# Second channel weights stored block by block from ScalarE, and the gated unit's spatial products one batch ahead of its output products, all on 128 rows

## The chip, the cores and the metric

The kernel runs on one core of a Trainium2 chip. The metric is the device time of one execution in microseconds (us). A core has TensorE (PE, with PEld for its weight loads), VectorE (DVE), ScalarE (ACT), GpSimd (POOL) and SyncE (SP, whose queue here issues DMAs). PEclk is the clock granted to TensorE, as a share of its upper level of 2.4 GHz; the lower level is 1.2 GHz, 0.5 in the rows.

## The reference, cut to what matters

Causal attention over 4 batches, 12 heads, 448 positions of 64, then a token and channel mixer with residuals, then a gated unit whose spatial product runs over the positions. Biases and weights are inputs; the five large weights arrive in 64 bits.

```python
attn = softmax(mask(q @ k.T / 8)) @ v                  # (4, 12, 448, 64)
x = attn.transpose(0, 2, 1, 3).reshape(4, 448, 768)
u = x + (relu(x.T @ w_tok1) @ w_tok2).T                # token mixing, 448 -> 256 -> 448
y = u + relu(u @ w_ch1) @ w_ch2                        # channel mixing, 768 -> 1536 -> 768
h = relu(y @ w_in)                                     # 768 -> 1024
g, v = h[..., :512], h[..., 512:]
v = (v - mean(v)) / sqrt(var(v) + 1e-6)
v = einsum('ts,bsd->btd', w_spatial, v) + b_spatial[None, :, None]
return (g * v) @ w_out                                 # 512 -> 768
```

## The kernel before, in words

**Numbers in two parts.** From the channel mixer on (and from the third batch of attention on), each factor is kept as a rounded high part and a low part that holds the rest (`split`, L78: the high part mostly on ScalarE, the low part on VectorE or GpSimd), and a product is three matmuls into one PSUM bank: high by high, high by low, low by high (`mm3`, L114, whose matmuls stand at L118 to L120). A 64-bit weight block is turned to 32 bits by three VectorE steps (`narrow_steps`, L99, steps at L103, L105 and L107).

**The scheduled part, L783 to L796.** Attention (24 pairs of heads, `pair_jobs`, 6 to a batch), token mixing (8 groups, `group_jobs`), the preparation of the channel weights (`weight_jobs`), the channel mixer (`channel_jobs`, one call to a batch) and the loads of the gated unit's input weights (`win_jobs`) are written as jobs with an engine, a cost, predecessors and a rank. `emit` (L213) is a list planner: it always takes the job that can start first by its own reckoning, and of those the one of lowest rank, and writes it out; each engine then runs its jobs strictly in that order. The table `RK` (L259) holds the rank offsets by kind of job, and `lag` (L261) the time that the planner puts between a job and its successor on another engine. So a change of any cost, rank or lag can reorder every engine.

**Weight blocks.** There are 24: 12 of `w_ch1` and 12 of `w_ch2`, each 128 x 768 numbers. One is loaded, narrowed by VectorE (tile `wn`), split by GpSimd (high part at L70, low part at L76) and stored to device memory, from which `channel_jobs` loads it again (tile `wb`, L670) once for each batch. `wn` and `wb` tiles share four slots (bank `w`: G4, G5, D2, D3). A `w_ch1` block is stored by one DMA (L622). A `w_ch2` block holds 128 rows of the hidden dimension and every output column, while the product wants 768 rows and 128 columns: so it is stored by two DMAs that scatter it in pieces of 512 bytes (L626), and a `wb` block of the second product waits for all six stores of its half (`src`, L673). The order of preparation is all of `w_ch1`, then all of `w_ch2`. Loads and stores all stand in SP's queue.

**Channel mixer.** For each batch and each half of the 1536 hidden columns there are six blocks of the first product (`cps<-uhl,wb`) and six of the second (`cps<-hid,wb`), each of 18 matmuls. In the first two batches' time the attention of the other two runs between these blocks.

**Gated unit, L802 to L951.** For each batch: four tiles of gate products (`psg`), then the value products of the three 128-row chunks (`value`, L818); after every second batch also one `value` call for the 64-row chunks of two batches together. Each value is normalised into `vn`. After the last batch, `normed(b)` (L885) splits the normalised values of a batch into high and low parts, `spatial(b)` (L903) multiplies them by the spatial weights (4 tiles of 11 matmuls), adds the bias and multiplies by the gate (L912, L913) and splits the result (`ghl`), and `project(b)` (L920) makes the output products (6 tiles of 12 matmuls) and stores them. The loop at L946 takes `spatial(b)`, `normed(b + 1)`, `project(b)` in turn. In `spatial` the 64-row chunk takes two matmuls: L908 multiplies a 128-row tile that has the high part in one half of its rows and the low part in the other by the high weights, which stand twice; L909 multiplies the high half alone, 64 rows, by the low weights. This part is written in program order, and the framework's own scheduler sets the order on each engine.

Of the kernel before, what the change touches and what calls it, by code (L numbers as in the profile page):

```python
# [16 lines left out]
DM = H * D  # L17
# [5 lines left out]
FF = 512  # L23
NG = FF // 128
CHUNKS = [(0, 64), (64, 192), (192, 320), (320, 448)]
MASKED = -1.0e9
# [5 lines left out]
def mixer_kernel(ctx: ExitStack, tc: tile.TileContext, qkv, wtok, w12, winu, winv, wsp, wout, bsp, out):  # L32
# [226 lines left out]
    RK = dict(s=39.4, q=-0.8, v=-43.0, e=22.5, pn=-59.8, f=5.8, hl=-47.5, pv=-27.9, ue=48.3, ut=-36.6, x=-71.7, h=56.7, hr=26.4, u=48.9, uc=37.6, us=19.6, ld=-6.7, ch=68.9, hd=-132.8, ad=33.2, nw=38.1, nh=39.6, wi=75.5)  # L259

    def lag(a, b):  # L261
        return 0.0 if a == b else 220.0 if a == "PE" else 80.0
# [326 lines left out]
    w2d = [dram.tile([KM, 128, 2, 6, 128], F32, tag=f"w2_{i}", name=f"w2_{i}") for i in range(2)]  # L589

    def weight_jobs(prev2):

        order = list(prev2)
        for x in range(2 * NF):
            i, f = x // NF, x % NF
# [8 lines left out]
            for s in range(3):  # L604
# [7 lines left out]
                at = Job("DVE", (900, 1500, 1350)[s], step, after=[at], rank=r + RK["nw"], bank=None if first else "w")  # L612
# [26 lines left out]
    def channel_jobs(b):  # L639
# [14 lines left out]
        for half_ in range(2):  # L654
# [6 lines left out]
            for x in range(12):  # L661
# [6 lines left out]
                def load(me, one=one, f=f, d=d, cell=cell, h=half_):  # L668
                    t = slot(me.tile, [2, DM], F32R, "wb")
                    nc.sync.dma_start(t.bitcast(F32), w1d[f] if one else w2d[h][d].rearrange("p t f c -> p t (f c)"))  # L670
# [172 lines left out]

    gates = []
    DO = {}
    for b in range(B):
# [10 lines left out]
        gates.append(g)  # L857
        for c in (1, 2, 3):
# [4 lines left out]
        if b == 0:  # L863
            for i in range(2):
                t = slot(f"D{turn('dbl', 4)}", [2 * S], F32, "wspt")
                nc.sync.dma_start(t, wsp[:, 2 * S * i : 2 * S * i + 2 * S])
                for c in range(2):
                    split(wsps[0][2 * i + c], wsps[1][2 * i + c], t[:, c * S : c * S + S], lo_eng="pool")
# [5 lines left out]
        if b == 3:  # L874
            for i in range(2):
                narrow(gates[2 + i][:, 4:6, :].rearrange("p f s -> p (f s)")[:, :DM], DO[1][i])
# [3 lines left out]
    for f in range(NG):  # L880
        t = slot(w12_slot(3 * (f // 2) + 1 + f % 2), [2, DM], F32R, f"wohl{f}")
        split(t[:, 0, :], t[:, 1, :], gates[f][:, 4:6, :].rearrange("p f s -> p (f s)")[:, :DM], lo_eng="pool")
        wo.append((t[:, 0, :], t[:, 1, :]))

    def normed(b):  # L885
        ns = []
        o = slice(64 * (b % 2), 64 * (b % 2) + 64)
        lo = slice(64 - 64 * (b % 2), 128 - 64 * (b % 2))
        t = slot(w12_slot(7), [3, FF], F32R, "nsh")
        x = vns[b // 2, 0]  # L890
        split(t[o, 0, :], t[lo, 0, :], x[o])
        ns.append((t[:, 0, :], t[o, 0, :]))
        ts = [t[:, 1, :], t[:, 2, :]]
        t = slot(w12_slot(8), [3, FF], F32R, "n8")
        ts += [t[:, i, :] for i in range(3)]
        t = slot(w12_slot(10), [3, FF], F32R, "n10")
        ts.append(t[:, 0, :])
        for c in (1, 2, 3):
# [119 lines left out]
```

## Time and profile before

| what | value |
|---|---|
| median of 3 runs | 902.36 us (901.5 to 902.97) |
| the profiled execution | 903.91 us, span 902.1 us, mean granted clock 0.987 |
| TensorE busy, share of the span | 863.0 us, 96% |
| VectorE, ScalarE, GpSimd busy | 423.8 us (47%), 300.7 us (33%), 284.1 us (31%) |
| TensorE's share of the chain that ended last | 80% |
| DMA | 148.65 MB, mean 165 GB/s |

The span runs from the first to the last instruction; the execution's own time holds 1.8 us more around it. Matmuls are pipelined, so TensorE counts as busy from the start of one to its modelled end, and a short pause between two matmuls can vanish in the busy time; the step from one matmul's start to the next shows it. The program has clear stages, so the tables by stage say more than the shares of the whole.

### The profile page before, as it was taken

What the parts mean: (1) busy time and instruction counts of PE and PEld (TensorE: products, weight loads), DVE (VectorE), ACT (ScalarE), POOL (GpSimd) and SP (SyncE); (2) the same over time, 40 slices, a digit from 0 to 9 for tenths busy, and PEclk for the clock granted to TensorE, in tenths of its full rate; (3) what the DMA queues carried; (4) which work ended last, traced back from release to release, by engine and by line L of the source; (5) the groups of instructions that cost most, each with busy time, mean ns of one, the idle gap of its engine ahead of it and who ended that gap; (6) DMA issues with size and microseconds to landing.
All of it is one profiled execution on the core that took longest, in us unless ns stands there. A gap on an engine that the chain in (4) does not pass through costs nothing.

```text
span 902.1 us, 12716 instructions
## 1 busy us (share of the span) xinstructions
PE 863.0 (96%) x4768; PEld 739.5 (82%) x4768; DVE 423.8 (47%) x775; ACT 300.7 (33%) x816; POOL 284.1 (31%) x376
## 2 busy tenths in 40 slices
PE   7899999886997999999999999999999999989998
PEld 5576777775996899989889999999998888877877
DVE  3787857754455334333452352322244355364342
ACT  5766565433323323333342201110204133322111
POOL 3589776646164231323313010101003000331020
PEclk9999999997999999999999999999999999999999
DMA  4686776877577855554255367677753000001111
GB/s 146 186 278 220 235 201 226 263 229 242 172 215 253 264 179 195 200 178 171 79 197 159 132 211 248 217 255 253 250 175 111 1 1 0 1 21 41 62 62 62
DMA packets 62701, 148.65 MB, mean 165 GB/s; under 512 B 17200, under 2 KB 40368, under 8 KB 62640
## 3 DMA queue, kind: packets, MB, share of 16 engines
q1 hardware_dynamic: 62640, 147.84, 49.9%
q8 instruction: 38, 0.62, 0.3%
q14 instruction: 23, 0.19, 0.1%
HBM read 123.44 MB, written 24.38 MB: 164 GB/s over the span
## 4 chain that ended last, share of the span: by engine, by line
PE 80%; DVE 6%; DMA 6%; POOL 4%; ACT 2%; issue 1%; SPq 0%; POOLq 0%; ACTq 0%; DVEq 0%
PE cps L118 13%; PE cps L120 12%; PE cps L119 12%; PE pst L405 4%; PE sa L350 3%; DMA w<-wn 3%; PE psg L120 2%; PE psg L119 2%; PE psg L118 2%; POOL pbig L392 2%; PE pso L436 2%; PE psv L118 2%; PE psv L119 2%; PE psv L120 2%; PE pso L119 2%; PE pso L120 2%
## 5 line engine op out<-in xcount | busy, mean ns | idle before, releaser
L118 PE MATMUL cps<-uhl,wb 128*128 128x448 f32 x288 | 109.4, 380 | 6.4 <-DMA wb<-w 2.9
L118 PE MATMUL cps<-hid,wb 128*128 128x448 f32 x288 | 108.8, 378 | 4.2 <-DMA wb<-w 4.2
L120 PE MATMUL cps<-hid,wb 128*128 128x448 f32 x288 | 106.5, 370 | 0.0
L119 PE MATMUL cps<-hid,wb 128*128 128x448 f32 x288 | 106.3, 369 | 0.0
L119 PE MATMUL cps<-uhl,wb 128*128 128x448 f32 x288 | 106.1, 368 | 0.0
L120 PE MATMUL cps<-uhl,wb 128*128 128x448 f32 x288 | 106.0, 368 | 0.0
L392 POOL TENSOR_SCALAR pbig<-pbig,rcp 128x448 f32<-128x448 f32 (+1 forms) x96 | 61.5, 650 | 108.6 <-DVE rcp L383 103.1
L83 DVE SCALAR_TENSOR_TENSOR hid<-cps,hid 128x448 fp32r<-128x448 f32 x48 | 29.9, 623 | 102.9 <-ACT hid L705 102.9
L377 ACT ACTIVATE pbig<-sa,nm 128x448 f32<-128x448 f32 (+1 forms) x72 | 42.6, 596 | 93.4 <-DVE nm L370 63.3
L713 DVE TENSOR_TENSOR U<-cps,U 128x448 f32<-128x448 f32 x48 | 29.9, 623 | 85.7 <-PE cps L120 85.1
L76 POOL TENSOR_TENSOR winl<-win,winh 128x1536 fp32r<-128x1536 f32 x4 | 14.8, 3695 | 171.4 <-ACT winh L68 139.5
L705 ACT ACTIVATE hid<-cps 128x448 fp32r<-128x448 f32 x48 | 26.1, 544 | 118.5 <-PE cps L120 118.5
L370 DVE TENSOR_REDUCE nm<-sa 128x2 f32<-128x896 f32 (+1 forms) x72 | 46.6, 679 | 38.8 <-PE sa L358 37.9
L118 PEld LDWEIGHTS cps<-uhl,wb 128*128 128x128 f32 x288 | 54.8, 190 | 12.1 <-issue 3.5
L118 PEld LDWEIGHTS cps<-hid,wb 128*128 128x128 f32 x288 | 54.9, 191 | 8.8 <-DMA wb<-w 4.3
L120 PEld LDWEIGHTS cps<-hid,wb 128*128 128x128 f32 x288 | 54.8, 190 | 4.7
L119 PEld LDWEIGHTS cps<-hid,wb 128*128 128x128 f32 x288 | 54.9, 191 | 4.3
L120 PEld LDWEIGHTS cps<-uhl,wb 128*128 128x128 f32 x288 | 54.6, 190 | 4.6
L119 PEld LDWEIGHTS cps<-uhl,wb 128*128 128x128 f32 x288 | 54.8, 190 | 3.8
L405 PE MATMUL pst<-ident,pbig 128*128 128x128 f32 x288 | 49.0, 282 | 4.6 <-POOL pbig L392 4.5
L76 POOL TENSOR_TENSOR wn<-wn 128x768 fp32r<-128x768 f32 x24 | 44.0, 1832 | 1.8
L392 POOL TENSOR_SCALAR psml<-psml,rcp 64x64 f32<-64x64 f32 (+1 forms) x96 | 43.2, 460 | 0.0
(184 smaller groups left out, 1951.7 us busy)
## 6 DMA issues: line engine op xcount, KB each, us to landing
wb<-w SPq DMA_DIRECT2D x96, 768.0 KB, 4.5
dbl<-in_w SPq DMA_DIRECT2D x24, 768.0 KB, 5.9
stage<-in_qkv SPq DMA_DIRECT2D x24, 448.0 KB, 4.1
w<-wn SPq DMA_DIRECT2D x12, 768.0 KB, 5.5
w<-wn SPq DMA_DIRECT2D x24, 384.0 KB, 8.2
out_t<-out SPq DMA_DIRECT2D x24, 224.0 KB, 1.9
dbl<-in_winu SPq DMA_DIRECT2D x4, 768.0 KB, 6.1
dbl<-in_winv SPq DMA_DIRECT2D x4, 768.0 KB, 6.8
```

Source lines behind the costliest of these rows:

```text
L76: e.tensor_tensor(lo, x, hi.bitcast(F32), op=ALU.subtract)
L83: nc.vector.scalar_tensor_tensor(lo, x, 0.0, hi.bitcast(F32), op0=ALU.max, op1=ALU.subtract)
L118: nc.tensor.matmul(ps, ah, bh, start=(first and i == 0), stop=False)
L119: nc.tensor.matmul(ps, ah, bl, start=False, stop=False)
L120: nc.tensor.matmul(ps, al, bh, start=False, stop=(last and i == n - 1))
L350: nc.tensor.matmul(out, x[rows, q0:q1], y[rows, S : 2 * S][:, ks[j]], start=(t == 0), stop=False, skip_group_check=True)
L370: nc.vector.tensor_reduce(nm[:M], S_.ps[:M, :, o : o + W], axis=mybir.AxisListType.X, op=ALU.max, negate=True)
L377: nc.scalar.activation(P(n, i)[:M, j, :], S_.ps[:M, j, o : o + W], AF.Exp, bias=SM[n, i][:M, j : j + 1], scale=1.0, accum_out=sums[n % 2][ ...
L392: nc.gpsimd.tensor_scalar(x, x, rcp[n % 2][:M, 2 * ((i - 1) % 4) + j :][:, 0:1], 1.0, op0=ALU.mult, op1=ALU.mult)
L405: nc.tensor.transpose(me.ps[:, o : o + M], src(), ident[:M, :M])
L705: nc.scalar.activation(part(x, 0), first.ps, AF.Relu)
L713: nc.vector.tensor_tensor(U[b][:, d, :], first.ps, U[b][:, d, :], op=ALU.add)
```

## The change

In `weight_jobs` the input layout of `w_ch2` is rearranged on the host so that a block already is what the second product wants (768 rows by 128 columns). Each `w_ch2` block is stored by one DMA like the others and a `wb` block waits for its own store alone. The blocks are prepared in the order six of `w_ch1`, six of `w_ch2`, six, six. All stores move from SP's queue to ScalarE's. The planner gets other costs, ranks and lags.

In the gated unit the 64-row matmul of L909 becomes one of 128 rows: its weights `wz` hold the low part in the half that belongs to the batch and zeros in the other. `normed(0)` moves ahead of the last batch's values and uses other slots; the loop becomes `spatial(0)`, `spatial(1)`, `project(0)`, `spatial(2)`, `project(1)`, `spatial(3)`, `project(2)`, `project(3)`; `project` no longer starts its first two tiles together.

```diff
+NARROW = (980, 1150, 1160)
-    RK = dict(s=39.4, q=-0.8, v=-43.0, e=22.5, pn=-59.8, f=5.8, hl=-47.5, pv=-27.9, ue=48.3, ut=-36.6, x=-71.7, h=56.7, hr=26.4, u=48.9, uc=37.6, us=19.6, ld=-6.7, ch=68.9, hd=-132.8, ad=33.2, nw=38.1, nh=39.6, wi=75.5)
+    RK = dict(s=53.0, q=-0.3, v=14.0, e=26.8, pn=-68.2, f=43.8, hl=-6.2, pv=-11.9, ue=33.0, ut=-111.3, x=-99.8, h=59.1, hr=-23.0, u=59.0, uc=55.2, us=45.6, ld=-58.4, ch=71.8, hd=-31.0, ad=-6.0, nw=76.8, nh=72.7, wi=295.1)
     def lag(a, b):
-        return 0.0 if a == b else 220.0 if a == "PE" else 80.0
+        return 0.0 if a == b else 220.0 if a == "PE" else 1500.0 if a in ("SP", "Q") else 80.0
...
-            i, f = x // NF, x % NF
+            i, f = x // 6 % 2, x % 6 + 6 * (x // NF)
...
-                if i == 0:
-                    nc.sync.dma_start(w1d[f], cell["w"].bitcast(F32))
-                else:
-                    for t in range(2):
-                        dst = w2d[f // 6][:, :, t, f % 6, :].rearrange("d p c -> p d c")
-                        nc.sync.dma_start(dst, cell["w"][:, t, :].bitcast(F32).rearrange("p (d c) -> p d c", c=128))
-            job(("st", i, f), "SP", 3300, store, after=[lo], rank=r + RK["nh"]).uses(first)
+                nc.scalar.dma_start((w1d, w2d)[i][f], cell["w"].bitcast(F32))
+            at2 = Job("ACT", 80, store, after=[lo], rank=r + RK["nh"])
+            job(("st", i, f), "Q", 3000, lambda _: None, after=[at2], rank=r + RK["nh"]).uses(first)
...
-                src = [("st", 0, f)] if one else [("st", 1, 6 * half_ + y) for y in range(6)]
+                src = [("st", 0, f)] if one else [("st", 1, 6 * half_ + d)]
-                L = job(("ld", b, i), "SP", 3300, load, after=[*src, *gate], rank=r + RK["ld"], bank="w")
+                L = job(("ld", b, i), "SP", 2500, load, after=[*src, *gate], rank=r + RK["ld"], bank="w")
...
+    wz = slot("q0", [2, S], F32R, "wz")
+    nc.gpsimd.memset(wz.bitcast(F32), 0.0)
...
+        tags = (w12_slot(7), w12_slot(8), w12_slot(10)) if b % 2 else ("D2", "D3", "D0")
...
+        if b == 3:
+            for i in range(2):
+                narrow(gates[2 + i][:, 4:6, :].rearrange("p f s -> p (f s)")[:, :DM], DO[1][i])
+            ns0 = normed(0)
...
-            nc.tensor.matmul(ps, ns[0][1][:, c], wsps[1][0][o], start=False, stop=False)
+            nc.tensor.matmul(ps, ns[0][0][:, c], wz[:, b % 2, :], start=False, stop=False)
...
-    ns = normed(0)
-    for b in range(B):
-        gs = spatial(b, *ns)
-        if b + 1 < B:
-            ns = normed(b + 1)
-        project(b, gs)
+    ns1 = normed(1)
+    gs = spatial(0, ns0)
+    split_out()
+    ns0 = normed(2)
+    gs1 = spatial(1, ns1)
+    project(0, gs)
+    ns1 = normed(3)
+    gs = spatial(2, ns0)
+    project(1, gs1)
+    gs1 = spatial(3, ns1)
+    project(2, gs)
+    project(3, gs1)
...
-    w12[:, :, DM:] = c2.reshape(NF, 128, DM)
+    w12[:, :, DM:] = c2.reshape(2, 6, 128, KM, 128).transpose(0, 3, 2, 1, 4).reshape(NF, 128, DM)
```

SP's queue of the kernel before, where the first half's second product begins in the first batch (`stage` is the next pair's attention input, `dbl` a 64-bit block, `wn` a prepared block, `w2_0` the stored `w_ch2` blocks of the first half, `wb` a block loaded again):

```order
L626 DMA w2_0_130<-wn_1945 128x6x128 x2
L93 DMA dbl_2199<-in_w12 128x1536
L286 DMA stage_84<-in_qkv 64x64
L287 DMA stage_84<-in_qkv 64x64
L294 DMA stage_84<-in_qkv 128x384
L282 DMA stage_84<-in_qkv 128x896
L626 DMA w2_0_130<-wn_2044 128x6x128 x2
L670 DMA wb_2260<-w2_0_130 128x1536
L670 DMA wb_2291<-w2_0_130 128x1536
```

The same place in SP's queue of the changed kernel:

```order
L94 DMA dbl_2095<-in_w12 128x1536
L667 DMA wb_2125<-w1_5_123 128x1536
L94 DMA dbl_2146<-in_w12 128x1536
L667 DMA wb_2181<-w2_0_130 128x1536
L94 DMA dbl_2214<-in_w12 128x1536
L667 DMA wb_2246<-w2_1_131 128x1536
L287 DMA stage_84<-in_qkv 64x64
L288 DMA stage_84<-in_qkv 64x64
L295 DMA stage_84<-in_qkv 128x384
L667 DMA wb_2295<-w2_2_132 128x1536
```

Before, the first load of a second-product block stands right behind the sixth store that it needs; in the change no store stands in this queue, the loads wait for one store each, and the 64-bit blocks stand between them.

ScalarE's order in the changed kernel before the channel mixer's first product (`qk` is the split of pair 12's scores' inputs, U a copy of attention's output, `xs` and `hid` are token mixing):

```order
L622 DMA w2_5_135<-wn_1392 128x1536
L622 DMA w1_6_124<-wn_1461 128x1536
L69 CAST qk_1550<-stage_84 128x896
L464 COPY U1_81<-pso_1521 128x448
L479 CAST xs_102<-psn_1567 64x128
L480 CAST xs_102<-psn_1567 128x3x128
L519 ACTIVATE hid_104<-psh_1561 128x384
L519 ACTIVATE hid_104<-psh_1588 128x384
```

Two stores now stand ahead of pair 12's split, where ScalarE had none. 18 of the 24 stores stand ahead of the first split of the channel mixer's input in this queue. In the same way VectorE narrows 18 blocks ahead of the low parts of that input where it narrowed 16, and GpSimd prepares 13 blocks ahead of pair 12's probabilities where it prepared 15.

ScalarE's order in the gated unit before (`ghl` is the split of a gated tile, `nsh` and `n8` are the next batch's `normed`, `out` the copies of output tiles):

```order
L68 CAST ghl_7057<-gt_7054 128x448
L68 CAST ghl_7075<-gt_7072 128x448
L68 CAST nsh_7114<-vn_6548 64x512
L68 CAST nsh_7114<-vn_6442 128x512
L68 CAST ghl_7093<-gt_7090 128x448
L68 CAST n8_7117<-vn_6442 128x512 x2
L68 CAST ghl_7111<-gt_7108 128x448
L942 COPY out_7151<-pso_7125 128x448
```

The same place in the change:

```order
L69 CAST ghl_7111<-gt_7108 128x448
L69 CAST ghl_7152<-gt_7149 128x448
L69 CAST ghl_7170<-gt_7167 128x448
L69 CAST nsh_7301<-vn_6994 64x512
L69 CAST nsh_7301<-vn_6768 128x512
L69 CAST ghl_7188<-gt_7185 128x448
L69 CAST n8_7304<-vn_6768 128x512
L69 CAST n8_7304<-vn_6994 128x512
L69 CAST ghl_7206<-gt_7203 128x448
L942 COPY out_7222<-pso_7209 128x448
```

Before, the first output tile follows the splits of its own batch; in the change the splits of the next batch (`ghl_7152` to `ghl_7206`) stand between.

## Rows read from the trace of the kernel before

**Rows 1.** Busy us, instructions, granted clock and DMA by stage.

```profile
core 0: us, PE busy (x) PEld busy (x) DVE busy (x) ACT busy (x) POOL busy (x), PEclk, DMA share, GB/s
0.00:174.24 174.24, 159.99 (x1004) 116.31 (x1004) 126.60 (x202) 103.24 (x332) 121.23 (x173) 1.00 0.69 219
174.24:300.00 125.76, 109.77 (x657) 96.48 (x657) 61.57 (x100) 38.71 (x113) 58.72 (x76) 0.92 0.74 226
300.00:671.70 371.70, 371.70 (x2108) 339.01 (x2107) 132.57 (x251) 96.36 (x252) 70.10 (x106) 1.00 0.58 196
671.70:788.75 117.05, 117.05 (x542) 101.37 (x541) 54.00 (x151) 39.48 (x78) 17.33 (x11) 1.00 0.09 30
788.75:898.40 109.65, 104.52 (x465) 86.36 (x464) 48.40 (x72) 22.87 (x43) 16.70 (x11) 0.98 0.13 49
```

**Rows 2.** TensorE's waits, 174 to 301 us (us in total, times, longest).

```profile
PE cps L118 <- DMA wb<-w: 7.1, 5, 4.2
PE sa L350 <- ACT psml L377: 3.4, 1, 3.4
```

**Rows 3.** The waits of SP's queue, whole span.

```profile
SPq L670 <- DMA w<-wn: 62.2, 13, 9.0
SPq L622 <- POOL wn L76: 6.7, 3, 4.9
```

**Rows 4.** DMA issues (KB each, median us to landing).

```profile
w<-wn SPq DMA_DIRECT2D x12, 768.0 KB, 5.5
w<-wn SPq DMA_DIRECT2D x24, 384.0 KB, 8.2
```

**Rows 5.** The stretches of low clock, columns as in rows 1.

```profile
190.00:195.00 5.00, 4.20 (x14) 3.83 (x15) 2.75 (x4) 1.93 (x8) 2.62 (x5) 0.66 0.33 84
215.00:230.00 15.00, 10.45 (x48) 9.47 (x49) 2.98 (x6) 2.28 (x11) 6.83 (x11) 0.57 0.56 199
290.00:300.00 10.00, 8.90 (x48) 7.28 (x47) 2.65 (x5) 3.21 (x6) 3.88 (x6) 0.83 0.96 284
```

**Rows 6.** Timeline of TensorE, spatial products of batch 0 (start us, us, instruction [idle before]).

```profile
790.72 0.52 PE L908 MATMUL psp<-hw,nsh 128*128 128x448 f32 x1 [1.79 <-DVE nsh L76]
...
797.55 0.37 PE L908 MATMUL psp<-hw,nsh 128*128 128x448 f32 x1
797.85 0.46 PE L909 MATMUL psp<-hw,nsh 64*128 64x448 f32 x1
...
798.55 0.37 PE L119 MATMUL psp<-hw,nsh 128*128 128x448 f32 x1
```

**Rows 7.** Timeline of TensorE, end of the last output products.

```profile
890.11 0.36 PE L120 MATMUL pso<-ghl,wohl 128*128 128x448 f32 x1
...
898.03 0.37 PE L120 MATMUL pso<-ghl,wohl 128*128 128x448 f32 x1
```

**Rows 8.** TensorE's waits, 788 to 903 us.

```profile
PE pso L119 <- DVE ghl L76: 3.3, 6, 0.6
```

**Rows 9.** Groups of instructions, 788.7 to 898.4 us (count, busy us, mean ns, idle before).

```profile
L913 DVE TENSOR_TENSOR gt<-gt,gate 128x448 f32<-128x448 f32 x16 | 13.2, 827 | 0.4
L76 DVE TENSOR_TENSOR ghl<-gt,ghl 128x448 fp32r<-128x448 f32 x16 | 12.9, 807 | 7.0 <-ACT ghl L68 7.0
L912 DVE TENSOR_TENSOR gt<-psp,bias 128x448 f32<-128x448 f32 x16 | 10.0, 625 | 10.8 <-PE psp L120 10.0
```

**Rows 10.** The weight blocks' own steps (duration ns min/median/max, first and last start).

```profile
L103 DVE TENSOR_SCALAR wn<-dbl x24: 549/666/4283, 40.3 to 283.7; 128x768 uint32<-128x768 uint32 x24
L105 DVE SCALAR_TENSOR_TENSOR wn<-dbl,wn x24: 942/960/2443, 40.9 to 285.4; 128x768 uint32<-128x768 uint32 x24
L70 POOL TENSOR_SCALAR wn<-wn x24: 821/830/1528, 43.3 to 290.9; 128x768 fp32r<-128x768 f32 x24
L76 POOL TENSOR_TENSOR wn<-wn x24: 1800/1826/1993, 44.2 to 291.8; 128x768 fp32r<-128x768 f32 x24
```

**Rows 11.** The `w_ch1` stores on SP's queue (duration of an issue as in rows 10).

```profile
L622 SPq DMA_DIRECT2D w<-wn x12: 326/384/1192, 47.1 to 135.7; - x12
```

More of the change, by code (lines that the diff above doesn't have):

```diff
@@ L588, in mixer_kernel @@
     w1d = [dram.tile([128, 2, DM], F32, tag=f"w1_{f}", name=f"w1_{f}") for f in range(NF)]
-    w2d = [dram.tile([KM, 128, 2, 6, 128], F32, tag=f"w2_{i}", name=f"w2_{i}") for i in range(2)]
+    w2d = [dram.tile([128, 2, DM], F32, tag=f"w2_{i}", name=f"w2_{i}") for i in range(2 * KM)]
     def weight_jobs(prev2):
@@ L610, in step @@
                     next(cell["g"])
-                at = Job("DVE", (900, 1500, 1350)[s], step, after=[at], rank=r + RK["nw"], bank=None if first else "w")
+                at = Job("DVE", NARROW[s], step, after=[at], rank=r + RK["nw"], bank=None if first else "w")
                 if first:
@@ L842, in value, with normed @@
         vns[key] = vn
+    wz = slot("q0", [2, S], F32R, "wz")
+    nc.gpsimd.memset(wz.bitcast(F32), 0.0)
+    def normed(b):
+        o = slice(64 * (b % 2), 64 * (b % 2) + 64)
+        lo = slice(64 - 64 * (b % 2), 128 - 64 * (b % 2))
+        tags = (w12_slot(7), w12_slot(8), w12_slot(10)) if b % 2 else ("D2", "D3", "D0")
+        t = slot(tags[0], [3, FF], F32R, "nsh")
+        x = vns[b // 2, 0]
+        split(t[o, 0, :], t[lo, 0, :], x[o])
+        ns = [(t[:, 0, :],)]
+        ts = [t[:, 1, :], t[:, 2, :]]
+        t = slot(tags[1], [3, FF], F32R, "n8")
+        ts += [t[:, i, :] for i in range(3)]
+        t = slot(tags[2], [3, FF], F32R, "n10")
+        ts.append(t[:, 0, :])
+        for c in (1, 2, 3):
+            split(ts[2 * c - 2], ts[2 * c - 1], vns[b, c], lo_eng="pool")
+            ns.append((ts[2 * c - 2], ts[2 * c - 1]))
+        return ns
     gates = []
@@ L873, in mixer_kernel, with split_out, spatial @@
             DO[1] = [fetch(half(wout[:, 1, :], i)) for i in range(2)]
-        if b == 3:
-            for i in range(2):
-                narrow(gates[2 + i][:, 4:6, :].rearrange("p f s -> p (f s)")[:, :DM], DO[1][i])
     wo = []
[L880 to L898, printed above, removed]
-            split(ts[2 * c - 2], ts[2 * c - 1], vns[b, c], lo_eng="pool")
-            ns.append((ts[2 * c - 2], ts[2 * c - 1]))
-        return ns, o
-    def spatial(b, ns, o):
+    def split_out():
+        for f in range(NG):
+            t = slot(w12_slot(3 * (f // 2) + 1 + f % 2), [2, DM], F32R, f"wohl{f}")
+            split(t[:, 0, :], t[:, 1, :], gates[f][:, 4:6, :].rearrange("p f s -> p (f s)")[:, :DM], lo_eng="pool")
+            wo.append((t[:, 0, :], t[:, 1, :]))
+    def spatial(b, ns):
         gs = []
@@ L920, in project @@
     def project(b, gs):
-        def products(ps, m, fs):
+        for m in range(KM):
+            ps = bank(4 + turn("v", 4), "pso")[:, :S]
             c = slice(128 * m, 128 * m + 128)
-            mm3(ps, [(wo[f][0][:, c], wo[f][1][:, c], *gs[f]) for f in fs], first=fs[0] == 0, last=fs[-1] == NG - 1)
-        pss = [bank(4 + turn("v", 4), "pso")[:, :S] for _ in range(2)]
-        for fs in (range(NG - 1), range(NG - 1, NG)):
-            for m in range(2):
-                products(pss[m], m, fs)
-        for m in range(KM):
-            if m < 2:
-                ps = pss[m]
-            else:
-                ps = bank(4 + turn("v", 4), "pso")[:, :S]
-                products(ps, m, range(NG))
+            mm3(ps, [(wo[f][0][:, c], wo[f][1][:, c], *gs[f]) for f in range(NG)])
             if m % 3 == 0:
```

11 lines of the change are left out of this document (9 added, 2 removed).

## The prediction

> **What bounds the kernel now.** I read the table by stage first [rows 1]. The bounds are where TensorE changes its work: at 174.24 us the first channel product starts, at 671.70 the first gate product, at 788.75 the last value product is over. From 300 to 788.75 us TensorE is busy without a gap at the full clock, and 489 of the 902 us can only change with the number of products, which the change leaves as it is there. The reader is to see that the time to be had lies in three other stretches. In 174.24 to 300 TensorE stands for 125.8 - 109.8 = 16.0 us, and its clock is 0.92. In 788.75 to 898.4 it stands for 5.1 us at 0.98. In 0 to 174.24 it stands for 14.2 us, while VectorE is busy 127, GpSimd 121 and ScalarE 103 of 174 us: there no engine is full, and attention's chain through all four sets the pace.
>
> Then I read who is waited for. In the second stretch it is mainly reloaded weights, and attention's single score bank: scores waited 3.4 us for ScalarE to read the scores ahead of them [rows 2]. SP's queue stood 62.2 us in 13 places at a reload until a store had landed [rows 3]. Six `w_ch2` blocks went out in 12 scattered half stores of 8.2 us each, where a whole `w_ch1` block takes 5.5 [rows 4].
>
> **The gated unit's end, term by term.** A steady product starts 0.203 us after the one before: (898.03 - 890.11) / 39 [rows 7]. In the spatial products the three starts from L908 to the matmul after the next take 1.00 us [rows 6], where three steady ones take 0.61. So the 64-row matmul costs 0.39 us more than its own step, in each of 16 places: 16 x 0.39 = 6.2 us, and as a 128-row matmul it should cost an ordinary step. The Trainium skill ("TensorE: Matmul & The Clock Gate", Part 2, step 3) says that throughput is purely the number of streamed columns; by that the 64-row matmul is no dearer and the swap is worth 0 instead of 6.2, a rival below. The same skill ("TensorEngine Tiling (Array Packing)", Key Properties) says that a switch of the tiling mode drains TensorE, and there the trace agrees, with these 0.39 us.
>
> The whole stage: 16 spatial tiles of 11 products and 24 output tiles of 12 make 464 products; 464 x 0.203 = 94.2 us, and 0.2 for the last one's length. The stage takes 109.65 [rows 1]. The difference, **15.2 us**, is the 6.2; the first wait of 1.8 [rows 6]; 3.3 us in six waits for the last split `ghl` of the batch [rows 8]; and 3.9 of slow clock behind the first wait and of restarts. I take all of it as gone:
> - The first wait ended with `normed(0)`. In the change that stands during the third batch's values, so TensorE goes straight on, and the clock has no reason to fall. `normed(1)`, which takes its place, is wanted 44 products, 8.9 us, later, and waited 1.8 us here.
> - Every `ghl` now has another batch's 44 products, 8.9 us, between it and its use.
> - The cover is VectorE's. A tile costs it 0.625 + 0.827 + 0.807 = 2.26 us [rows 9], and TensorE 11 x 0.203 = 2.23. Two spatial products in a row leave VectorE behind by a fraction of a us and by two 64-row splits; the 14.6 us of output products after them, with three copies, catch that up. If they did not, the next tile of the same bank would wait, some 2 us for each pair.
>
> The earlier narrowing of the last output weights, GpSimd's two 64-row low parts and the cleared tile lie in the stage where GpSimd is busy 17 and VectorE 54 of 117 us [rows 1]: 0. The splits of the output weights stay between the last gates: 0.
>
> **The first channel blocks, 174 to 300 us.** 16.0 us of standing and the slow clock are to be had. A clock of 0.66 over 5 us means 3.4 us at half speed, 0.57 over 15 us 12.9, 0.83 over 10 us 3.4 [rows 5]; less the standing in those stretches (0.8, 4.55, 1.1) that is 2.6, 8.35 and 2.3 us of work done at 1.2 GHz, which half the time would have done: 6.6 us. Together 22.6. The clock fell where TensorE had just stood, so it comes back with the waits.
>
> What takes the waits away: the second product's first block waits for its own store rather than for the last of six; the six blocks that it needs are prepared as numbers 7 to 12 instead of 13 to 18; and 24 products stand between pair 13's two score groups, which followed each other before. What stays: the four `w` slots still serve both the preparation and the reloads, and five or six blocks are still prepared during the first half's first product. A block holds a slot for two VectorE steps of 0.96 and one of 0.67, for GpSimd's 0.83 + 1.83 [rows 10] and for a store of 5.5 [rows 4], so 10.8 us at least; six of them with six reloads in four slots nearly fill that part, 108 products or 21.9 us and the attention of about one pair between them. I leave 7 of the 22.6 us there: gain **15.6 us**, bounds 0 (the slots and transfers set it all) and 22.6.
>
> **Attention, 0 to 174 us.** The order changes on every engine, and no row prices an order. Ahead of the first product VectorE now narrows two blocks more, 2 x 2.59 = 5.2 us [rows 10]; GpSimd has two fewer ahead of pair 12's probabilities, 2 x 2.66 = 5.3 us earlier; ScalarE issues 18 stores, 18 x 0.384 = 6.9 us [rows 11], out of 71 us in which it is idle [rows 1]. SP loses as much. I take **0**, for no engine is full; the bounds are +12 (all of VectorE's and ScalarE's on the path) and -9 (all of TensorE's waits but the first 4.7 us load).
>
> **Sum.** -15.2 - 15.6 + 0 = -30.8. The profiled execution took 903.9 us, of which 1.8 lie around the span; so 873.1 for such a run. It stands 1.5 us above the median of the runs, 902.4, which makes **871.5 us**.
>
> **The rivals.**
> 1. All waits of the first channel blocks go: 7 us more, 864.5. For it: later batches run the same mix of blocks and attention with none [rows 1]. Against it: no weights are prepared then. Chance 0.12.
> 2. The transfers and slots set the pace there whatever the order, and the waits stay: 871.5 + 15.6 = 887. For it: DMA engines are busy 0.74 of that stretch and 0.96 at 290 to 300 [rows 1, 5]. The Trainium skill ("DMA: Bandwidth & Descriptors", Issuing engines are not separate DMA queues) says that issuing from several engines saves the issue time only; it would allow this case. Against it: in the worst stretch, 215 to 230, DMA was at 0.56 [rows 5]: the wait was for an order, not for bytes. Chance 0.20.
> 3. **Slower: ScalarE stands at the stores.** Each store waits in ScalarE's strict order for GpSimd's low part, with exponentials, splits and copies of attention behind it, for which TensorE waits. SP came too early for a store three times, by 4.9 us at most [rows 3]. If each of the 18 stores ahead of the channel mixer meets its low part just begun, ScalarE loses 18 x (1.83 + 0.38) = 39.8 us; with the other terms as above that is 911. It decides from 30.8 / 18 - 0.38 = 1.3 us of wait for each store, passed on in full. Against it: ScalarE is idle for 0.4 of the stage, and the order puts most stores behind copies that themselves wait for TensorE. Chance 0.04.
> 4. The 16 products keep their extra 0.39 us, since the pause belongs to this place and not to the 64 rows: 877.7. Against it: every other 128-row matmul around it takes one step. Chance 0.04.
>
> **How the numbers follow.** The forecast has the rest, 0.60. The range takes in rivals 1, 2 and 4 with some us of the unknown order of attention at both ends: 861 to 889. About 0.2% (1.8 us) is what a measurement of this kernel tells from no change. Only rival 3, or rival 2 with attention's worst bound, comes near the old time: faster 0.95, same 0.01, slower 0.04.
>
> **What would show it.** Right: the spatial stage to the last product takes some 95 us at a clock of 1.00, with no wait at its first product and none for `ghl`; L908 and its follower stand one step apart; TensorE's idle time between the first channel product and the end of attention falls from 16 to some 5 us, and SP's waits for stores nearly vanish. Wrong: ScalarE waiting for GpSimd's `wn` in the first 174 us, a first channel product later than about 180 us, or waits for `wb` as long as before.

## The result and the profile after

The changed kernel takes **889.12 us** (median of 4 runs, 887.16 to 893.45), beside it the kernel before 902.31: a ratio of 0.986, interval 0.983 to 0.988. It is faster by 13.2 us, less than half of the 30.8 forecast, and just outside the range of 861 to 889. The profiled execution took 889.3 us, span 887.5. One execution of each kernel is profiled, and executions of one kernel differ by some us, in time and granted clock: here 887.16 us at a mean clock of 0.992 and 893.45 at 0.983.

The table by stage of the changed kernel, columns as in [rows 1]; the bounds are again the first channel product, 300 us, the first gate product, and the first and last product of the gated unit's end:

```profile
0.00:187.20 187.20, 165.46 (x1004) 120.12 (x1004) 137.20 (x209) 102.92 (x332) 131.06 (x177) 0.96 0.69 231
187.20:300.00 112.80, 106.19 (x648) 93.75 (x648) 56.06 (x87) 35.66 (x107) 51.01 (x63) 0.97 0.64 228
300.00:672.60 372.60, 371.31 (x2116) 338.09 (x2115) 137.88 (x257) 99.49 (x259) 76.75 (x116) 1.00 0.56 192
672.60:789.60 117.00, 117.00 (x541) 101.28 (x541) 55.52 (x152) 41.44 (x82) 22.39 (x14) 1.00 0.07 22
789.60:884.00 94.40, 94.40 (x465) 86.96 (x464) 45.47 (x71) 20.74 (x39) 12.29 (x9) 1.00 0.15 57
```

The last row is what was forecast: 94.40 us, TensorE never stands, full clock. From the first gate product to the span's end it is now 887.5 - 672.6 = 214.9 us, and was 902.1 - 671.9 = 230.2: **15.3 us less**. From the first channel product to the first gate product it is 485.4 us and was 497.7: 12.3 less. But the first row is 13.0 us longer, with the same 1004 TensorE instructions in it: TensorE stands for 21.7 us there instead of 14.2, and its clock is 0.96 instead of 1.00. So the first gate product comes at 672.6, not earlier than before (671.9). All of the net gain is the gated unit's; the weights' part won 12 us in the channel blocks and lost 13 in attention.

Who is waited for in the changed kernel, by engine (us in total, times, longest): TensorE up to 187 us and from 187 to 300, ScalarE up to 300, SP's queue up to 320, GpSimd up to 187 us:

```profile
PE pst L406 <- POOL pbig L393: 7.0, 7, 2.2
...
PE cps L119 <- DMA wb<-w: 5.1, 3, 3.8
...
ACT pbig L378 <- POOL wn L77: 10.5, 2, 5.7
...
SPq L94 <- DVE wn L108: 45.1, 13, 8.7
SPq L667 <- DMA w<-wn: 37.4, 8, 9.5
...
POOL stage L323 <- DMA stage<-in_qkv: 19.8, 9, 8.4
```

And the stores among its DMA issues, as in [rows 4]:

```profile
w<-wn ACTq DMA_DIRECT2D x24, 768.0 KB, 5.3
```

The 24 stores now go out whole and land in 5.3 us at the median. The rows for `cps` and of SP at L667 answer to [rows 2, 3]: less waiting for reloaded blocks and for stores, and none is left for the scores ahead. New is ScalarE at a store behind GpSimd's low part. The other waits have grown: in the kernel before, TensorE up to 174 us, SP's queue up to 320 and GpSimd up to 174 had

```profile
PE pst L405 <- POOL pbig L392: 2.7, 4, 1.1
...
SPq L93 <- DVE wn L107: 7.2, 3, 4.2
...
POOL stage L322 <- DMA stage<-in_qkv: 11.1, 7, 4.2
```

Of the 7.5 us that TensorE stands longer ahead of the first channel product, 4.3 are waits for GpSimd's probabilities (`pbig`).

How one of these comes about, from 63 to 75 us of the changed kernel, in the timelines of VectorE, GpSimd and TensorE (start us, us, instruction [idle before]):

```profile
66.56 1.11 DVE L106 SCALAR_TENSOR_TENSOR wn<-dbl,wn 128x768 uint32<-128x768 uint32 x1
67.59 1.78 DVE L383 TENSOR_SCALAR rcp<-sums 128x8 f32<-128x8 f32 x1
...
66.30 0.56 POOL L323 TENSOR_SCALAR stage<-stage 128x448 f32<-128x448 f32 x1 [0.54 <-DMA stage<-in_qkv]
66.83 2.51 POOL L77 TENSOR_TENSOR wn<-wn 128x768 fp32r<-128x768 f32 x1
69.78 1.77 POOL L393 TENSOR_SCALAR pbig<-pbig,rcp 128x448 f32<-128x448 f32 x2 [0.45 <-DVE rcp L384]
...
73.82 0.55 PE L406 MATMUL pst<-ident,pbig 128*128 128x128 f32 x3 [1.80 <-POOL pbig L393]
```

A weight block's low part stands on GpSimd just ahead of the probabilities; VectorE's first small step of the reciprocals, 0.16 us in its shortest execution, lasts 1.78 and ends with that low part; then come the probabilities, and TensorE has stood 1.80 us.

### The profile page after: what moved, and what is told of

The parts are those of the page before. It is cut to its first block, busy times and chain, and to the rows that moved or that the text cites. A ratio compares the mean times of both kernels' runs of the same rounds, so it can differ in the third digit from the quotient of the medians.

```text
span 887.5 us, 12703 instructions
## 1 busy us (share of the span) xinstructions
PE 854.4 (96%) x4768; PEld 740.2 (83%) x4768; DVE 432.8 (49%) x775; ACT 300.3 (34%) x816; POOL 293.5 (33%) x378
## 4 chain that ended last, share of the span: by engine, by line
PE 83%; POOL 6%; DVE 4%; DMA 3%; ACT 2%; issue 2%; ACTq 0%; POOLq 0%; SPq 0%
PE cps L119 13%; PE cps L120 12%; PE cps L121 12%; PE pst L406 4%; PE sa L351 3%; PE pso L437 3%; PE psg L120 2%; PE psg L121 2%; PE psg L119 2%; PE pso L121 2%; PE pso L119 2%; PE pso L120 2%; PE psv L119 2%; PE psv L120 2%; PE psv L121 2%; POOL pbig L393 2%
## 5 line engine op out<-in xcount | busy, mean ns | idle before, releaser
L393 POOL TENSOR_SCALAR pbig<-pbig,rcp 128x448 f32<-128x448 f32 (+1 forms) x96 | 65.1, 687 | 90.6 <-DVE rcp L384 85.3
L119 PEld LDWEIGHTS cps<-hid,wb 128*128 128x128 f32 x288 | 54.1, 188 | 8.0 <-DVE U L710 2.3
L121 PEld LDWEIGHTS cps<-hid,wb 128*128 128x128 f32 x288 | 54.1, 188 | 4.6
L120 PEld LDWEIGHTS cps<-hid,wb 128*128 128x128 f32 x288 | 54.2, 188 | 4.1
L77 POOL TENSOR_TENSOR wn<-wn 128x768 fp32r<-128x768 f32 x24 | 46.3, 1928 | 1.6
L406 PEld LDWEIGHTS pst<-ident,pbig 128*128 128x128 f32 x288 | 35.0, 142 | 12.7 <-POOL pbig L393 11.2
```

What stands on the lines that cost most here:

```text
L77: e.tensor_tensor(lo, x, hi.bitcast(F32), op=ALU.subtract)
L119: nc.tensor.matmul(ps, ah, bh, start=(first and i == 0), stop=False)
L120: nc.tensor.matmul(ps, ah, bl, start=False, stop=False)
L121: nc.tensor.matmul(ps, al, bh, start=False, stop=(last and i == n - 1))
L393: nc.gpsimd.tensor_scalar(x, x, rcp[n % 2][:M, 2 * ((i - 1) % 4) + j :][:, 0:1], 1.0, op0=ALU.mult, op1=ALU.mult)
L406: nc.tensor.transpose(me.ps[:, o : o + M], src(), ident[:M, :M])
```

## The experiments

Two theories at the start. S: ScalarE, standing at stores, made attention longer. N: it is the narrowing, or the order of the new table. First the change was cut in two and the stores moved.

**One: the gated unit alone.** All lines above the gated unit's as before.

> The kernel before with the change's gated unit alone (the cleared tile, the 128-row product, the spatial products one batch ahead); weights and planner as before. Theory 1 (the gated unit gave all of the gain, the weights nothing): the stage from the last value product on falls from 113.3 us to about 98, the time to 902.3 - 15.2 = 887, within 2 us. Rival (the gated unit gave less and the weights some of the 13): 890 to 896.

Measured: 888.96 us, ratio 0.987 (0.984 to 0.989). From the first gate product to the end 888.1 - 673.1 = 215.0 us. The gated unit gave all of the gain.

**Two: the weights' part alone.** The mirror.

> The changed kernel with the gated unit of the kernel before: block stores from ScalarE, new order and new table alone. Theory 1 (idle time moved from the channel blocks into attention, none was lost): first channel product near 187 us, first gate product near 672, time 902 to 905, the same as before within 0.3%. Rival (the weights gain some 5 to 10 us, which something in the changed gated unit costs again): 892 to 897.

Measured: 905.52 us (898.1 to 910.9 in 10 runs), ratio 1.004 (1.001 to 1.008). Theory 1, with 902 to 905, comes nearest: alone, the weights' part makes the kernel a little slower. The profiled execution took 900.0 us, with its first channel product at 183.7 us and its first gate product at 668.1.

**Three and four: the stores on other queues.**

```diff
-                nc.scalar.dma_start((w1d, w2d)[i][f], cell["w"].bitcast(F32))
+                nc.sync.dma_start((w1d, w2d)[i][f], cell["w"].bitcast(F32))     # three
+                nc.gpsimd.dma_start((w1d, w2d)[i][f], cell["w"].bitcast(F32))   # four
```

> The changed kernel with the 24 stores issued from SP's queue instead of ScalarE's, at the same place of the program, all else in the same order. Theory S (ScalarE standing at stores behind GpSimd's low part, 10.5 us in two places on the store's successor, is what made attention longer): first channel product 5 to 13 us earlier than 187, time 877 to 884. Rival N (what made it longer is the narrowing of weight blocks on VectorE ahead of attention's small steps, and the stores are beside the path): first channel product near 187, time 887 to 891. Third (SP stands at the stores with the loads of queries, keys and weights behind it): later than 889.

> The changed kernel with the 24 stores issued from GpSimd's own queue, at the same place of the program, behind the low parts that they store, so that no other engine waits for them. Theory S (ScalarE's waits at the stores made attention longer): 877 to 884, unless the issue on GpSimd itself costs much. Rival N (VectorE's narrowing made it longer): 887 to 891. If an issue costs GpSimd over 1 us, 18 of them ahead of the first channel product lie on an engine that is busy 131 of 187 us, and the time could rise by up to 18 us.

Measured: 890.94 us (ratio 0.989, 0.985 to 0.994) from SP, 893.39 (0.993, 0.990 to 0.995) from GpSimd; the first channel product at 193.4 and 189.7 us. Nothing is won by taking the stores away from ScalarE, where theory S had 5 to 13 us. But each queue then pays a price of its own. SP stands at the stores behind the low parts (up to 200 us):

```profile
SPq L622 <- POOL wn L77: 32.5, 10, 6.6
```

And GpSimd spends 0.60 us on each of the 18 issues ahead of the first channel product, 10.8 us in all. So these two runs alone don't settle S; run five adds to them.

**Five: the old table.** Everything of the change stays but the planner's ranks, its lags and the three narrowing costs.

```diff
-NARROW = (980, 1150, 1160)
+NARROW = (900, 1500, 1350)
-    RK = dict(s=53.0, q=-0.3, v=14.0, e=26.8, pn=-68.2, f=43.8, ...
+    RK = dict(s=39.4, q=-0.8, v=-43.0, e=22.5, pn=-59.8, f=5.8, ...
-        return 0.0 if a == b else 220.0 if a == "PE" else 1500.0 if a in ("SP", "Q") else 80.0
+        return 0.0 if a == b else 220.0 if a == "PE" else 80.0
```

> The changed kernel with the planner's table, lags and narrowing costs of the kernel before: block layout, one store each from ScalarE, blocks in turns of six and the gated unit stay. Theory R (the new table put weight work ahead of attention's steps and that alone made the first channel product 13 us later): first channel product at 174 to 178, the channel blocks keep their gain of some 12 us, time 875 to 880. Rival W (the new order of blocks itself asks for it, whatever the table): first channel product after 183, time 886 to 893.

Measured: **872.84 us**, ratio 0.969 (0.966 to 0.972). Theory R has it, by more than it forecast: taking the table back gives 16 us. Its reason doesn't hold, though: ahead of the first channel product VectorE narrows 19 blocks under the old table and 18 under the new one, so the new table did not put more weight work there. The stages, columns as in [rows 1]:

```profile
0.00:177.50 177.50, 159.94 (x1003) 116.37 (x1004) 144.25 (x211) 101.92 (x331) 138.40 (x179) 1.00 0.74 248
177.50:300.00 122.50, 118.74 (x729) 106.09 (x729) 59.97 (x101) 41.64 (x119) 49.99 (x69) 1.00 0.65 230
300.00:655.60 355.60, 355.60 (x2037) 323.99 (x2036) 130.84 (x240) 94.02 (x247) 71.67 (x108) 1.00 0.56 192
```

GpSimd's waits up to 177.5 us, TensorE's and ScalarE's up to 300:

```profile
POOL stage L323 <- DMA stage<-in_qkv: 7.3, 5, 4.2
...
PE pst L406 <- POOL pbig L393: 3.2, 5, 1.5
...
ACT U L464 <- POOL wn L77: 5.4, 4, 1.9
ACT xs L479 <- POOL wn L77: 4.9, 1, 4.9
```

VectorE and GpSimd are fuller than in the changed kernel (144 and 138 us of 177.5), TensorE still stands less and has the full clock throughout. The first gate product comes at 655.6 us, 17.0 earlier. Up to there the products are the same, and TensorE was busy 634.3 us and stood 21.3; with the new table it was busy 643.0 and stood 29.6 (before the change 641.7 and 30.2). So 8.3 of the 17 us are waits, and 8.7 are longer busy time of the same products, in one execution at a clock of 0.98 up to there and one at 1.00. The clock isn't all of it: the kernel of run two has the same program as the changed one up to the gated unit, its execution had a clock that rounds to 1.00 up to its first gate product, and that still came at 668.1, 12.5 us after the old table's.

ScalarE stands 10.3 us behind GpSimd's low parts with the old table too (10.5 in the changed kernel), ahead of copies instead of exponentials. So its standing by itself isn't the price; with runs three and four that speaks against theory S.

**Six: more buffers for the fetches.** Twelve halves go in turn to D0, D1 and two buffers that attention needs only later.

```diff
-                cell["d"] = fetch(half(w12[f], i), 2)
+                cell["d"] = fetch(half(w12[f], i), 2, ("D0", "D1", "G11", "G12")[x % 4] if x < 12 else None)
```

> The changed kernel with the first twelve weight halves fetched into four buffers in turn instead of two (the two others are idle until attention's pair 12 uses them), no instruction in another place. SP stood 36.4 us in 12 places at a fetch until VectorE had narrowed the block two before (7.2 us in 3 before the change), with attention's loads behind it; GpSimd waited 19.8 us for those loads (11.1 before). Theory F (these stands made attention longer): that wait falls under 10 us, first channel product 5 to 12 us earlier than 187, time 878 to 885. Rival D (VectorE and GpSimd, sharing the narrowing and the splits, set the pace): SP's wait goes, but the first channel product stays at 184 to 189, time 887 to 892.

Measured: 890.34 us, ratio 0.988 (0.984 to 0.992); the first channel product at 195.3 us in an execution of 897.1 us. SP's waits from 30 to 187 us in it:

```profile
SPq L287 <- PE pso L437: 41.7, 9, 13.3
...
SPq L94 <- DVE wn L108: 22.8, 5, 9.5
```

SP stands less at fetches and more at the next entry, loads of values whose buffer TensorE has not left (20.0 us in the changed kernel). GpSimd's wait for loads did not fall (17.5 us from 30 us on, and 14.7). Theory F falls.

**Seven and eight: a shorter narrowing,** in the changed kernel and, as control, in the old front with the new gated unit.

```diff
-        nc.vector.scalar_tensor_tensor(w, hi, 0xC0000000, w, op0=ALU.bitwise_and, op1=ALU.bitwise_or)
+        if not short:
+            nc.vector.scalar_tensor_tensor(w, hi, 0xC0000000, w, op0=ALU.bitwise_and, op1=ALU.bitwise_or)
```

> The changed kernel without the second of the three narrowing steps of each channel weight block (the two top bits, sign and highest exponent bit, are left out of the weights, so the output is another one); no other instruction moves. It takes 18 x 1.29 = 23 us from VectorE ahead of the first channel product. Theory D (the narrowing beside attention's steps sets attention's pace in the changed kernel): first channel product 8 to 15 us earlier than 187, time 874 to 882. Rival F (SP's stands at fetches): some 3 to 6 us earlier, since each fetch then waits a little less. If it is only order: within 2 us.

> The kernel before with the changed gated unit, and without the second narrowing step of each channel weight block (so the output is another one): the counterpart of the run above in the old order. It takes 16 x 1.11 = 17.8 us from VectorE ahead of the first channel product. Theory D: here the narrowing lay beside the path, so the first channel product moves by less than 4 us from 175 and the distance to the changed kernel without that step shrinks from 12 us to under 5. Rival (order alone): the distance stays at 10 to 13 us.

Measured: 880.33 us (0.977, 0.973 to 0.980) and 881.91 (0.980, 0.975 to 0.984): 8.8 and 7.1 us less than with the step. The first channel product moved from 187.2 to 176.7 us and from 175.9 to 170.9, so the distance shrank from 11 to 6, between the two expectations. Narrowing lies on the path in either order. By the time it costs both nearly the same, so it isn't what sets the two kernels apart; of the 11 us between their first channel products it makes up 5.

**Nine and ten: which half of the table.** The changed kernel with old lags and narrowing costs, and with old ranks.

> The changed kernel with its own ranks, but the planner's lags and narrowing costs of the kernel before. Taking ranks, lags and costs all back gave 872.8 us. Theory K (the ranks cost the 16 us): still 886 to 892, first channel product after 183. Rival L (the lag of 1.5 us behind transfers and the narrowing costs did it): 871 to 876, first channel product before 180. In between: both, or the parts of the table only fit each other.

> The changed kernel with the ranks of the kernel before, but its own lags and narrowing costs: the mirror of the run above. Theory K (ranks): 871 to 876. Rival L (lag and costs): 886 to 892.

Measured: 902.70 us (1.001, 0.998 to 1.003) and 881.20 (0.977, 0.973 to 0.980). The four corners:

| | old lags and costs | new lags and costs |
|---|---|---|
| old ranks | 872.8 | 881.2 |
| new ranks | 902.7 | 889.1 |

The ranks lose in both columns, 30 and 8 us. The new lags and costs mend 14 us of what the new ranks lose, and lose 8 with the old ranks. Neither theory had the price, and a part of the table has none without the rest.

Nor is the first channel product a measure of the loss. It came at 194.3 us with the old lags and costs (with 37 TensorE instructions fewer ahead of it), and at 187.9 with the old ranks: as late as in the changed kernel (187.2), in a kernel that is 8 us faster. New lags and costs alone bring attention's whole delay, then. What the new ranks add to them lies behind it: from the first channel product to the first gate product it is 477.2 us with the old ranks and 485.4 with the new ones.

**Eleven: the block layout alone,** in the old order with the new gated unit. One store for each block from SP, the second product waits for its own block. The planner has two edges more: a second product's block starts after the last block of the first, and a batch after the start of the last block of the one before.

> The kernel before with the changed gated unit and, of the weights' part, the block layout alone: one store for each block from SP, the second product waits for its own block; old order of blocks (twelve and twelve), old table. Theory B (the turns of six are what lets the second product start in time): the waits between 200 and 300 us stay, time 883 to 889 where the changed gated unit alone gives 889. Rival C (own stores are enough): the channel blocks gain 10 us or more, time 873 to 880.

Measured: 886.48 us, ratio 0.983 (0.979 to 0.987), beside 888.96 without the layout: no more than a few us, by intervals that overlap. The rest of the way to 872.8 comes with the turns of six, the stores from ScalarE and the planner's costs of stores and loads, which weren't tried apart. (In its profiled execution, of 890.6 us, waits between the first channel product and 300 us fell to 8.6 us, and attention had a clock of 0.97. That the waits stay was wrong.)

**Twelve and thirteen: GpSimd's stand at the loads,** in the changed kernel and with the old table.

```diff
-nc.gpsimd.tensor_scalar(q, q, 0.125, 1.0, op0=ALU.mult, op1=ALU.mult)
+None
```

> The changed kernel without GpSimd's scaling of the queries by 1/8 (it is left out, so the scores and the output are others); nothing else moves. In the changed kernel GpSimd stands 14.7 us in 7 places at that instruction until the load lands, with the scaling of probabilities and the low parts queued behind it; with the old table it stands 2.2 us. Theory G (this standing is what the new ranks cost): first channel product 8 to 14 us earlier than 187, time 875 to 881. Rival O (the order on TensorE costs it, GpSimd's stand is beside the path): time 885 to 889, some 2 to 4 us less for the 14 instructions of 0.62 us that GpSimd is spared.

> The same left out of the changed kernel with the old table, as a control. Theory G: 1 to 4 us less than 872.8, since GpSimd hardly stood there, so that the distance between the two tables shrinks from 16 to 4 to 10 us. Rival O: the same 2 to 4 us in both, the distance stays at 14 to 18.

Measured: 881.96 us (0.980, 0.977 to 0.983) and 870.92 (0.967, 0.964 to 0.969). It takes 7.2 us from the one and 1.9 from the other (0.5 beside run eighteen), and the distance shrinks from 16 to 11. Theory G has the direction and a third of the size: some **5 us** of the 16 are GpSimd standing at a load with probabilities and low parts behind it.

**Fourteen and fifteen: whose ranks.** The changed kernel with attention's ranks as before, and with all others as before.

> The changed kernel with its own lags and costs, the ranks of attention's steps (loads, scores, exponentials, probabilities, transposes, products) as in the kernel before, all other ranks new. All ranks new: 889; all old: 881.2. If attention's ranks make GpSimd stand at the loads: 879 to 883, that wait under 8 us. If the others do: 887 to 891.

> The mirror: the ranks of token mixer, weights and channel blocks as before, those of attention's steps new. If attention's ranks are to blame: 887 to 891, GpSimd's wait at the loads 12 us or more; if the others: 879 to 883.

Measured: 885.13 us (0.982, 0.980 to 0.984) and 893.22 (0.991, 0.988 to 0.994), between 889.1 and 881.2 for all or none and beyond. Attention's old ranks bring 4 us, the other old ranks alone lose 4, both together bring 8. GpSimd's wait at the loads from 20 us on fell to 6.5 and 6.1 us, in the second although the time rose, where TensorE waited 12.0 us for GpSimd's probabilities instead of 7.0. So that stand alone doesn't rank the orders.

**Sixteen to eighteen: a version beyond both.** With the old table, the queries' scale goes into the exponential; then ScalarE copies the high parts too.

```diff
+                nc.vector.tensor_scalar_mul(nm[:M], nm[:M], 0.125)
-... bias=SM[n, i][:M, j : j + 1], scale=1.0, ...
+... bias=SM[n, i][:M, j : j + 1], scale=0.125, ...
-            hi = Job("POOL", 1000, ... "pool"), after=[at]      # seventeen
+            hi = Job("ACT", 850, ... "act"), after=[at]
```

> The changed kernel with the old table, the scaling of the queries by 1/8 moved from GpSimd into the exponential: ScalarE's scale is 0.125, and VectorE multiplies the 96 negated maxima (128x2) by 0.125; the output is the reference's. Leaving the scaling out alone gave 1.9 us. If GpSimd's time counts: 869 to 872. If VectorE's small steps on the way from score to exponential count more (some 0.1 us each, four for each pair): 874 to 880.

> As the run above, and the high part of each weight block is copied by ScalarE instead of GpSimd (24 times 0.83 to 1.5 us); the planner places the step anew. If GpSimd bounds attention: 864 to 870. If ScalarE then stands at the narrowing with attention's exponentials behind it, or the new order costs more than it gives: 873 to 885.

> The changed kernel with the old table once more, beside the two runs above: 872 to 874 as before.

Measured: 882.74 us (0.979, 0.976 to 0.982), 901.41 (1.001, 0.999 to 1.003), and 871.44 (0.966, 0.962 to 0.971) for the old table. Both sixteen and seventeen are slower than either of their expectations. The best version stays the changed kernel with the old table, 29 us below the kernel before. Why sixteen loses: the new small step, its executions in ns (shortest, median, longest):

```profile
L372 DVE TENSOR_SCALAR nm<-nm x96: 159/170/2257, 8.0 to 500.4; 128x2 f32<-128x2 f32 x72, 64x2 f32<-64x2 f32 x24
```

And those on 128 rows ahead of the first channel product, at 186.7 us (busy us, mean ns | idle before):

```profile
L372 DVE TENSOR_SCALAR nm<-nm 128x2 f32<-128x2 f32 x39 | 17.9, 460 | 1.3
```

Sparing GpSimd 14 instructions of 0.6 us isn't worth 52 small steps between maximum and exponential, at 0.17 us each at the median and 0.43 on average in attention (17.9 us for 39, and 4.3 for the 13 of 64 rows). Thirteen, which leaves the scaling out and puts nothing in its place, took 870.92: the small steps cost 11.8 us. In seventeen ScalarE stands at the narrowing, and GpSimd behind ScalarE (waits of ScalarE from 20 us, of GpSimd, up to the first channel product at 211.9 us):

```profile
ACT wn L69 <- DVE wn L108: 16.4, 7, 5.6
...
POOL wn L77 <- ACT wn L69: 20.2, 6, 7.9
```

## Why the prediction was wrong

- **The gated unit's end: right.** Forecast -15.2 us; 15.3 and 15.2 less in two pairs of traces. The 464 products were to take 94.2 + 0.2, and took 94.4. No first wait, no wait for `ghl` [rows 6, 8]. The product that had 64 rows keeps step with its neighbours now (start us, us, instruction):

```profile
789.65 0.37 PE L919 MATMUL psp<-hw,nsh 128*128 128x448 f32 x1
789.86 0.36 PE L920 MATMUL psp<-wz,nsh 128*128 128x448 f32 x1
790.06 0.37 PE L119 MATMUL psp<-hw,nsh 128*128 128x448 f32 x1
```

  The rule weighed against it, that only streamed columns count (the Trainium skill, "TensorE: Matmul & The Clock Gate", Part 2), is at odds with these rows: the columns are the same 448, and the step fell from 0.39 us too much to none. The time of the 128-row product by itself, without the batch ahead, wasn't measured.
- **The first channel blocks: right in kind.** Forecast -15.6, bounds 0 and 22.6; with the new table -12.3, with the old one 497.7 - 478.1 = 19.6. With the new table 5.1 us of waits for reloaded blocks stayed (7.1 in [rows 2]); with the old one, on the same four slots, none did, so the 7 us that I left to the slots were too much there.
- **Attention: the step that failed.** "I take 0, for no engine is full". It cost 13.0 us, beyond the worst bound of 12 and more than the channel blocks won. VectorE was busy 10.6 us longer in that stretch and GpSimd 9.8, where I had counted 5.2 and nothing; but with the old table both are busier still, so that isn't what cost it. A busy share says nothing about which instruction stands ahead of which in a strict order. The change carried a whole new set of ranks, lags and costs, and I priced them at nothing because no row prices an order; the old table under the same change gives 872.8, and only 3.3 us of attention's 13. That this is within 1.3 us of my 871.5 is in part luck: the channel blocks gave 4.0 us more than I took, attention 3.3 less. My bounds were built from added work alone (narrowing, stores), and left out waiting and the clock.
- **Rival 2 gave 887 and for the wrong reason.** Transfers and slots don't set the pace: the same stores and slots under the old table give 872.8.
- **Rival 3 was half seen.** ScalarE did stand behind GpSimd's low part, 10.5 us in two places, not at all 18 stores, and moving the stores away didn't help.
- **The signs I named** held: ScalarE waiting for `wn`, and a first channel product later than 180 us, were said to show the forecast wrong. Of the signs for right, the spatial stage came as said; TensorE's idle time from the first channel product on fell from 16.0 to 7.9 us, not to some 5; and SP's waits for stores fell from 62.2 [rows 3] only to 37.4.

Shown: the table costs 16 us; some 5 us of it pass through GpSimd's stand at the query loads. Part of it is slow clock, but how much isn't fixed by the order: 12.5 us stood between the first gate products of two executions whose clock up to there rounds to 1.00. Open: which places of the order cost the other 11. The ranks work only as a set, and no single wait among those tried accounts for them.

## What to carry to other kernels

A change that comes with a new set of scheduling numbers is two changes: price it with the old numbers too, and run that version, since here it was worth more than the whole edit. Where several in-order engines are each some three quarters busy, don't take a reordering as free: bound its cost by the idle time and slow clock that the best and the worst order of the same work show, not by the work that moves. And measure the clock's part in more than one execution. And a step moved to an engine with idle time can still lose, if it lands between a maximum and its exponential.

## What the hardware showed that I had not expected

**The same stands cost more clock in one execution than in another.** Stretches of 5 us of the changed kernel, columns as in [rows 1]:

```profile
70.00:75.00 5.00, 2.56 (x13) 1.57 (x11) 4.50 (x6) 2.01 (x7) 5.00 (x7) 1.00 0.84 254
75.00:80.00 5.00, 4.98 (x29) 3.48 (x30) 0.98 (x1) 2.20 (x6) 4.70 (x6) 0.66 0.51 159
130.00:135.00 5.00, 2.76 (x14) 1.75 (x12) 4.89 (x7) 1.94 (x8) 5.00 (x6) 1.00 0.82 260
135.00:140.00 5.00, 4.35 (x28) 3.40 (x27) 0.86 (x2) 1.36 (x3) 4.92 (x6) 0.68 0.90 330
```

Twice TensorE stands 2.2 to 2.4 us of five, and then runs in part at 1.2 GHz; so it does twice more, after 165 and after 205 us. With the old table it stands 0.6 to 2.0 us in each of four such stretches in a row, and the clock stays at 2.4 GHz:

```profile
140.00:145.00 5.00, 4.27 (x28) 3.37 (x27) 3.01 (x2) 3.13 (x7) 4.92 (x6) 1.00 0.91 320
145.00:150.00 5.00, 4.44 (x20) 2.65 (x20) 4.86 (x6) 1.20 (x4) 5.00 (x8) 1.00 0.44 176
150.00:155.00 5.00, 4.04 (x34) 3.37 (x34) 4.22 (x3) 0.47 (x1) 4.86 (x3) 1.00 0.73 219
155.00:160.00 5.00, 2.99 (x16) 2.79 (x16) 3.94 (x7) 3.31 (x12) 4.81 (x5) 1.00 1.00 332
```

4.3 us of waiting spread over 20 us cost no clock there, and 2.2 us in one stretch did above. That looks like a matter of the order, but it isn't of the order alone. Run two has the same program up to the gated unit, and at the same places:

```profile
70.00:75.00 5.00, 3.06 (x13) 1.80 (x12) 4.93 (x6) 1.71 (x8) 5.00 (x7) 1.00 0.78 234
75.00:80.00 5.00, 4.32 (x26) 2.88 (x27) 1.20 (x2) 2.20 (x6) 4.92 (x6) 0.75 0.73 220
130.00:135.00 5.00, 3.62 (x14) 1.80 (x12) 4.92 (x7) 2.99 (x11) 5.00 (x6) 1.00 0.89 334
135.00:140.00 5.00, 3.35 (x29) 2.55 (x29) 2.10 (x3) 1.36 (x3) 4.92 (x6) 1.00 0.92 302
```

From 130 to 140 us TensorE stands 3.0 us here and keeps the full clock; in the changed kernel it stood 2.9 and lost it. So in these traces neither the sum of the waits nor their place in the order tells what they cost in clock, and one execution of each of two kernels doesn't compare their clocks.

**A tiny VectorE step can last as long as a GpSimd instruction.** The reciprocals' first step took 0.16 us at its shortest and 1.78 beside a low part, and the two ended within 0.03 us of each other (the rows from 63 to 75 us above). The low part itself took 2.51 us where its median is 1.84: it began while a narrowing step had 0.8 us to go. And the 128x2 step of sixteen took 0.17 at the median and 2.26 at the longest. The Trainium skill ("SBUF — State Buffer", Who interferes with whom) says that VectorE and GpSimd share a pair of ports, and that when a VectorE instruction runs in a mode that uses both pairs, as a `tensor_scalar` can, whichever of the two engines comes first holds the shared pair for its whole instruction and the other is blocked. The trace agrees, with the two ends together; which mode these steps ran in it doesn't show.
